# Two attention heads' kernels in one launch: another order of the first loads, and another rule for which engine copies

## The chip, the cores and the metric

The kernel runs on one core of one Trainium2 chip. A core has five engines with instruction queues of their own: PE (matrix multiplies; PEld is its weight load), DVE (vector), ACT (scalar, with table functions such as Exp), POOL (GpSimd) and SP (issues DMAs here). They wait for each other through semaphores. SBUF is the working memory of 128 partitions; PSUM, which PE writes, has 8 banks of 128 x 512 float32. The metric is the device time of one launch in microseconds (us), lower is better.

## The reference

Two blocks over inputs of 2048 rows by 512 columns, 32 heads of 16 columns each, their outputs side by side:

```python
def _A_ref(x, wqkv, wo):
    ...
    scores = jnp.einsum("bhqd,bhkd->bhqk", q, k) * scale
    p = _softmax(scores, axis=-1)
    o = jnp.einsum("bhqk,bhkd->bhqd", p, v)
    return ... @ wo
def _B_ref(x, wqkv, w_phi, wo):
    ...
    pq = jnp.einsum("bhsd,hdf->bhsf", q, w_phi)
    pk = jnp.einsum("bhsd,hdf->bhsf", k, w_phi)
    phi_q = jnp.concatenate([_softmax(pq, axis=-1), _softmax(-pq, axis=-1)], axis=-1)
    phi_k = jnp.concatenate([_softmax(pk, axis=-1), _softmax(-pk, axis=-1)], axis=-1)
    ...
    o = num / den
    return ... @ wo
return jnp.concatenate([a, b], axis=-1)
```

Block A, full softmax attention over 2048 x 2048 scores for each of 32 heads, is nearly all of the work; B is attention with linear cost.

## The kernel before

The kernel computes A's scores twice. Once with queries on the partitions (line L1050), in blocks of 128 queries by 512 keys, for which DVE takes the row maximum out of PSUM (L1058, one or two banks at once). The maxima, negated, are then put into spare rows of the query tile QT, so that the second time, with keys on the partitions (L1144), the scores come out with the maximum already subtracted, and ACT takes Exp into pT (issued in the helper at L402). PE multiplies pT with V (L1210) and with ones for the sums. There are 2048 blocks on either side. They are grouped in units: four heads by 128, 256 or 512 queries. The maxima of a unit must be complete before its first Exp; DVE runs ahead of ACT by what the code calls the lead. For the first four units a part of the maxima is taken pairwise: the score difference of two key chunks (L969), Relu by ACT, and an add with maximum on DVE (L1004).

At the start x is loaded to SG (L489), turned by PE with an identity matrix (L619, copied out by ACT and DVE in turn, L627), and then K and Q are projected: K for the first two groups by `proj_kq` (PE L533, ACT writes KT), Q for the first 128 and the next 384 queries by `first_q` (PE L575, DVE L582 and ACT). The first score block needs both. K's mask columns (kmask, kone) and the identity are made by POOL. `load_w` (L485) loads the weights' first columns: K's on SP's queue, Q's on ACT's. Later projections, block B's work and the output projections are "jobs", run by PE between the scores; copies out of PSUM follow on ACT.

No order is written out by hand. While the program is built, a planner walks through an estimated time of its own and gives each engine its next instruction: for PE in `try_pe` (queued work, then maxima or exps by how full DVE's and ACT's queues are, then products with V, jobs, and last fillers, matmuls of ones with zeros that keep the activity of PE at a set share, L1446, L1461, L1468), for the others in `try_eng` (lowest `prio` first). A copy by ACT may have an alternative on DVE (`n.alt`); `try_eng` gives it to DVE when all maxima are done or when the lead is over `K.LEAD` units. The planner's weights (`_Knobs.SPAN`) are drawn anew for each 36 us of its time, from a seed in `SEEDS0`.

Of the kernel before, what the change touches and what calls it, by code (L numbers as in the profile page):

```python
# [139 lines left out]

P0 = 0.5
W0 = 0.4


class _Knobs:
    SPAN = (("FILL", FM, FL, FH), ("FROW", 0.1, 0.0, 0.2), ("FDUP", 0.0, -0.03, 0.05), ("LCOL", 0.03, 0.0, 0.08),
# [3 lines left out]
            ("PC", 0.03, 0.0, 0.2), ("DS", 0.3, 0.05, 0.7), ("WE", W0, 0.1, 0.8), ("JN", 0.0, -0.05, 0.05),  # L150
# [30 lines left out]
def bass_concat_heads__softmax_full_mha__linear_kernel_hedgehog__prompt_kernel(  # L181
# [10 lines left out]
    RING = 28  # L192
    DT = 36
    KM = 2
    JT = 18
    SEG = 36
    SEEDS0 = [339, 17, 597, 940, 351, 78996, 101, 127, 545, 311, 973669, 597, 812, 52566, 422803204, 815, 523,
              407, 428, 535419061790, 532, 532941, 587, 227, 532591402781660, 622774033, 610, 622774292, 587,
              48, 23, 550, 382, 177996]
    VB = 7  # L200
# [20 lines left out]
    with contextlib.ExitStack() as es:  # L221
# [156 lines left out]

        log = []

        def start(n):
# [73 lines left out]
        def parity(dst, t, key, src, prio):  # L455
            pool(lambda e: e.tensor_tensor(pt4[:], t[:, 0:4], t[:, 4:8], ALU.add), 0.22, [src], ["pt4"], prio=prio)
            pool(lambda e: e.tensor_tensor(dst[:], pt4[:, 0:2], pt4[:, 2:4], ALU.add), 0.22, ["pt4"], [key],
                 prio=prio)

        blocks(hmask, "hmask", 15, 0)  # L460
        parity(kmask, hmask, "kmask", "hmask", 0)
# [26 lines left out]
        for t in range(4):  # L488
            dma("xn%d" % t, lambda e, t=t: e.dma_start(SG[:, t, :], A_x[0][128 * t:128 * t + 128, :]), (),  # L489
                [("SG", t)], prio=0, us=0.45, land=3.2, q="act" if t % 2 else "sp")  # L490
# [16 lines left out]
        pool(lambda e: e.memset(ident[:], 1.0), 0.1, (), ["ident"], prio=0)  # L507
        pool(lambda e: e.affine_select(
            ident[:], ident[:], pattern=[[-1, 128]], base=0, channel_multiplier=1,
            compare_op=ALU.is_ge, fill=0.0), 0.3, (), ["ident"], prio=0)  # L510
        pool(lambda e: e.affine_select(
            ident[:], ident[:], pattern=[[1, 128]], base=0, channel_multiplier=-1,
            compare_op=ALU.is_ge, fill=0.0), 0.3, (), ["ident"], prio=0)

# [504 lines left out]
        def try_m1_of(u, sm, single):  # L1019
# [403 lines left out]
        def try_fill():  # L1423
# [34 lines left out]
            if mode != "full":  # L1458
                if not pe_ok("col"):
                    return False  # L1460
                pe_op([lambda e, q=q: e.matmul(  # L1461
                    PS[32 * q:32 * q + 32, VB, :], ones_t[:, 0:32], zmv[:, :],
                    tile_position=(0, 32 * q), **kw) for q in range(4)], vdeps, "col")
            else:
                if not pe_ok("full"):
                    return False
                cw = 128 if now < COLD else 512
                pe_op([lambda e: e.matmul(PS[:, VB, 0:cw], ones_t[:, :], zmv[:, 0:cw], **kw)], vdeps, "full", None, (),  # L1468
                      cw / 2400.0)
# [6 lines left out]
        def try_pe():  # L1476
# [8 lines left out]
            if m1["u"] >= NU:  # L1485
# [9 lines left out]
                if pv_soon():  # L1495
                    return False
            for e in (("dve", "act") if d <= a + K.DA else ("act", "dve")):
                if e == "dve" and d < K.TM and try_m1(d < K.DS):
# [110 lines left out]


        def to_dve(n, w):
            now = state["now"]
            return r1_nodes and m1["u"] < NU and now > 1040.0 and lead() > 0.5 and free["dve"] <= w + 0.5

        def try_eng(k):
            now = state["now"]
            best = None
            for n in waiting[k]:
                w = n.when()
                if w is not None and w <= now + 1e-6 and (  # L1620
                        best is None or (n.prio, n.seq) < (best.prio, best.seq)) and not (
                            k == "act" and n.alt is not None and to_dve(n, w)):
                    best = n
            if k == "dve" and (m1["u"] >= NU or lead() > K.LEAD):
                for n in waiting["act"]:
# [5 lines left out]
                if best is not None and best.eng == "act":  # L1631
                    waiting["act"].remove(best)
                    best.eng = "dve"
                    best.run, best.occ, best.lat = best.alt
                    waiting["dve"].append(best)
# [127 lines left out]
```

## Time and profile before

| | us |
|---|---|
| three executions | 1238.96, 1210.88, 1210.67 |
| median | 1210.88 |
| the profiled execution | 1211.18 |
| its span, first to last instruction | 1209.4 |

The granted TensorE clock of that execution is 1.000. In the profile, instructions that are merged in one row have a start, a length and a count; a name such as `KT<-PS` is tile written, tile read; the number behind `<-` in brackets is idle time and who ended it. The costliest group beside those shown further down is ACT's Exp of 128 x 512 elements, 2038 times, 1055.6 us in total. The mean of a row includes the part by which an instruction overlaps the next on its engine.

### The profile page before, as it was taken

The numbers are of one execution on the slowest core, as the hardware profiler recorded it, in microseconds if no ns is written. First come the engines' busy times: TensorE is split into PE (matmuls) and PEld (weight loads), VectorE is DVE, ScalarE is ACT, GpSimd is POOL, SyncE is SP. The second block draws the span as 40 slices with busy tenths as digits, with TensorE's granted clock in tenths as the row PEclk, the third lists the DMA queues.
The fourth block names the chain that finished last, engine by engine and source line by source line (L and its number), as shares of the span: only waits on it lengthen the run. The fifth ranks groups of instructions, "written<-read, shape, count | busy, mean of one in ns | idle before, by whom it ended". The sixth has DMA issues, their size and how long they took to land.

```text
span 1209.4 us, 39536 instructions
## 1 busy us (share of the span) xinstructions
PE 1186.3 (98%) x16833; PEld 569.1 (47%) x16833; DVE 1173.3 (97%) x1195; ACT 1174.2 (97%) x2393; POOL 838.9 (69%) x1193
## 2 busy tenths in 40 slices
PE   8999999999999999999999999999999999999998
PEld 4453344444434444455444344545445434455565
DVE  6999999999999999999999999999999999999993
ACT  7899999999999999999999999999999999999998
POOL 5168988879876676678888979889898896311120
PEclk9999999999999999999999999999999999999999
DMA  9200010001000100010111211111111111000000
GB/s 201 41 12 6 7 26 9 8 7 26 9 11 22 27 7 8 9 25 17 27 32 36 46 23 33 35 26 25 25 26 26 28 40 24 14 13 9 10 12 21
DMA packets 98561, 30.48 MB, mean 25 GB/s; under 512 B 85328, under 2 KB 98384, under 8 KB 98384
## 3 DMA queue, kind: packets, MB, share of 16 engines
q1 hardware_dynamic: 97424, 27.49, 11.9%
q8 instruction: 132, 2.16, 0.7%
q10 hardware_dynamic: 960, 0.46, 0.1%
q14 instruction: 45, 0.37, 0.1%
HBM read 4.73 MB, written 4.19 MB: 7 GB/s over the span
## 4 chain that ended last, share of the span: by engine, by line
ACT 48%; PE 28%; DVE 22%; POOL 1%; issue 1%; DMA 0%; ACTq 0%; DVEq 0%; POOLq 0%
ACT pT L402 42%; DVE part L1058 21%; PE PS L1144 8%; PE PS L1050 5%; PE PS L1446 4%; PE PS L1210 3%; PE PS L533 2%; ACT eB L402 2%; PE PS L701 1%; ACT pB L402 1%; PE PS L607 1%; PE PS L1461 1%; ACT xAT L402 1%; ACT X L402 1%; PE PS L778 1%
## 5 line engine op out<-in xcount | busy, mean ns | idle before, releaser
L1058 DVE TENSOR_REDUCE part<-PS 128x2 f32<-128x1024 f32 (+1 forms) x1043 | 1146.6, 1169 | 9.3 <-PE PS L1050 3.8
L402 ACT ACTIVATE pT<-PS 128x512 bf16<-128x512 f32 x2038 | 1055.6, 692 | 15.5 <-PE PS L1144 9.3
L1144 PE MATMUL PS<-QT,KT 32*128 32x256 bf16 (+1 forms) x4480 | 696.9, 262 | 8.6 <-ACT pT L402 1.3
L1446 PE MATMUL PS<-zmv,ones_t 32*128 32x256 bf16 x3638 | 583.2, 271 | 1.1 <-ACT pB L402 0.7
L1050 PE MATMUL PS<-KT,QT 32*128 32x512 bf16 x2533 | 483.9, 382 | 3.5 <-DVE part L1058 1.7
L1144 PEld LDWEIGHTS PS<-QT,KT 32*128 32x128 bf16 x4480 | 241.7, 92 | 271.3 <-ACT pT L402 187.5
L1446 PEld LDWEIGHTS PS<-zmv,ones_t 32*128 32x128 bf16 x3638 | 275.3, 92 | 36.0 <-ACT X L402 3.6
L1210 PE MATMUL PS<-pT,VP 128*17 128x256 bf16 (+1 forms) x4480 | 193.3, 265 | 1.2 <-ACT xAT L402 0.4
L1050 PEld LDWEIGHTS PS<-KT,QT 32*128 32x128 bf16 x2533 | 124.1, 91 | 123.7 <-issue 51.5
L1271 POOL TENSOR_TENSOR lr<-lr,cons 128x8 f32<-128x8 f32 (+1 forms) x66 | 104.7, 1587 | 43.6 <-DMA lr<-X 43.5
L1210 PEld LDWEIGHTS PS<-pT,VP 128*17 128x17 bf16 x4480 | 69.1, 88 | 95.0 <-issue 81.6
L821 POOL TENSOR_TENSOR den_t<-den_t,cons 128x32 f32<-128x32 f32 x16 | 87.2, 5448 | 0.2
L741 POOL TENSOR_TENSOR sB<-eB 128x512 f32<-128x512 bf16 x32 | 36.9, 1152 | 58.6 <-ACT eB L402 58.6
L728 POOL TENSOR_SCALAR sB<-sB 128x256 f32<-128x256 f32 (+2 forms) x96 | 68.8, 717 | 6.5
L1108 POOL TENSOR_SCALAR stage<-mrow 128x8 bf16<-128x8 f32 (+1 forms) x64 | 15.3, 240 | 82.0 <-DVE mrow L1084 81.7
L1281 POOL TENSOR_TENSOR QT<-X,Yd 128x256 bf16<-128x256 f32 (+1 forms) x66 | 45.8, 693 | 35.4 <-DMA Yd<-Yd 35.4
L764 POOL TENSOR_TENSOR wA<-eB,rB 128x1024 bf16<-128x1024 bf16 x32 | 61.7, 1927 | 11.7 <-ACT rB L402 11.6
L726 POOL TENSOR_TENSOR sB<-uB 128x256 f32<-128x256 f32 (+2 forms) x96 | 45.7, 476 | 5.8
L570 POOL TENSOR_SCALAR KT<-SG,kmask,kone 128x512 bf16<-128x512 bf16 x27 | 20.5, 769 | 30.0 <-ACT SG L402 30.0
L730 POOL TENSOR_TENSOR uB<-sB,uB 128x256 f32<-128x256 f32 x64 | 37.8, 591 | 3.4
L744 POOL TENSOR_TENSOR sB<-sB 128x256 f32<-128x256 f32 x64 | 36.1, 563 | 3.1
L1461 PE MATMUL PS<-zmv,ones_t 128*32 128x512 bf16 x408 | 36.9, 386 | 0.0
(131 smaller groups left out, 866.9 us busy)
## 6 DMA issues: line engine op xcount, KB each, us to landing
Yd<-Yd SPq DMA_DIRECT2D x232, 16.0 KB, 2.1
out_dram<-xAT SPq DMA_DIRECT2D x16, 128.0 KB, 1.7
out_dram<-OA SPq DMA_DIRECT2D x15, 128.0 KB, 1.7
QT<-mcols SPq DMA_DIRECT2D x116, 2.0 KB
QT<-in_A_x_dram SPq DMA_DIRECT2D x2, 512.0 KB, 6.7
mcols<-stage SPq DMA_TRANSPOSE x64, 2.3
lr<-X SPq DMA_DIRECT2D x58, 4.0 KB
Yd<-lr SPq DMA_DIRECT2D x58, 4.0 KB
```

Source lines behind the costliest of these rows:

```text
L402: n = mk("act", lambda ds: P.op("act", lambda e: e.activation(out_(), in_(), func, **kw), ds), reads, writes, deps, occ=c + (0.093 if sbuf ...
L728: pool(lambda e, w=w: e.tensor_scalar(sB[:, 0:64 * w], sB[:, 0:64 * w], 1.0, 0.0, ALU.mult, ALU.max), us1, ["sB"], ["sB"])
L764: pool(lambda e: e.tensor_tensor(phiB[k].rearrange("p (g f) -> p g f", f=16), e3, rB[:, i, :].unsqueeze(2).broadcast_to([128, 64, 16]), AL ...
L821: pool(lambda e: e.tensor_tensor(den_t[:, :], den_t[:, :], cons[:, 0:32], ALU.pow), 5.42, ["cons"], ["den"])
L1050: fns = [lambda e, rr=rows[i], b=banks[i]: e.matmul(PS[:, b, :], QT[32 * rr:32 * rr + 32, g, q0 + 128 * qt:q0 + 128 * qt + 128], KT[32 * r ...
L1058: d = dve(lambda e: e.tensor_reduce(part[:, ub, off + m:off + m + k], PS[:, banks[0]:banks[-1] + 1, :], AX.X, ALU.max), 512 * k, (), (), d ...
L1144: fns = [lambda e, kt=kg * ns + j, j=j: e.matmul(PS[:, bank, j * nq:(j + 1) * nq], KT[32 * r:32 * r + 32, g, kt * 128:(kt + 1) * 128], QT[ ...
L1210: fns.append(lambda e, r=r, s=s, kt=kt, j=j: e.matmul(PS[32 * r:32 * r + 17, VB, 0:nq], VP[:, kt, 8 * (g // 2) + 2 * r + g % 2, :], pT[:, ...
L1271: pool(lambda e: e.tensor_tensor(lr[:, ub, 0:nr], lr[:, ub, 0:nr], cons[:, 0:nr], ALU.pow), 0.17 * nr + 0.2, ["cons"], [("lr", ub)], prio=2)
L1281: mul_nodes[u] = pool(lambda e, a=a: e.tensor_tensor(QT[:, g, q0 + a:q0 + a + w], X[:, ub, a:a + w], Yd[:, ub, a:a + w], ALU.mult), w * 0. ...
L1446: n = pe_op([lambda e, r=r: e.matmul(PS[:, VB, 0:FW], ones_t[32 * r:32 * r + 32, :], zmv[32 * r:32 * r + 32, 0:FW], tile_position=(32 * r, ...
L1461: pe_op([lambda e, q=q: e.matmul(PS[32 * q:32 * q + 32, VB, :], ones_t[:, 0:32], zmv[:, :], tile_position=(0, 32 * q), **kw) for q in rang ...
```

## The change

Five edits go together:

1. The three POOL instructions that make the identity stand ahead of the masks (they stood after the loads), all with the same `prio`.
2. Q's first weights go to SP's queue, behind K's, instead of ACT's. The K projection of the first two groups gets a lower (earlier) due time, -0.6, than Q's -0.5.
3. While the planner's time is under 20 us (`WT`), if a maximum's score block could start on PE within 0.21 us and DVE is about free, `try_pe` issues nothing else.
4. Fillers stay 128 columns wide until 9.0 us (`CW`) instead of 6.5.
5. A copy changes from ACT to DVE when the work that ACT has left exceeds DVE's by more than `K.SH` us, drawn between -1 and 9 (`behind`), and no more by the lead.

The planner's estimates of some times (load landings, identity steps) are changed too, and `SEEDS0` is another list, so all later order is planned afresh.

```diff
+S0 = 4
...
-            ("TA", 3.0, 1.2, 3.0), ("LB", 1.7, 0.6, 2.4), ("LEAD", 1.5, 1.0, 2.5), ("DA", 0.4, -0.4, 1.0),
+            ("TA", 3.0, 1.2, 3.0), ("LB", 1.7, 0.6, 2.4), ("SH", S0, S0 - 5.0, S0 + 5.0), ("DA", 0.4, -0.4, 1.0),
...
+    OT = 148
+    WT = 20
+    KF = 1
+    CW = 9.0
...
-    SEEDS0 = [339, 17, 597, 940, 351, 78996, 101, 127, 545, 311, 973669, 597, 812, 52566, 422803204, 815, 523,
+    SEEDS0 = [825, 789, 964, 663, 278, 663475996, 876, 847819, 103, 666322, 337517, 337517559, 666322306588,
...
+            if n.eng == "act":
+                if n.prio == 4:
+                    tally["e"] += len(n.frees)
+                else:
+                    tally["other"] += n.occ
             for pool, b in n.frees:
+                if pool == "m":
+                    tally["m"] += 2 if len(n.frees) == 1 and n.occ > 0.61 else 1
...
+        pool(lambda e: e.memset(ident[:], 1.0), 0.1, (), ["ident"], prio=0)
+        pool(lambda e: e.affine_select(
...
         blocks(hmask, "hmask", 15, 0)
...
-                [("SG", t)], prio=0, us=0.45, land=3.2, q="act" if t % 2 else "sp")
-        load_w("wk0", ("wA", 1, 0), 512, 640, 4.4, "sp", 0)
-        load_w("wq0", ("wA", 0, 0), 0, 128, 4.4, "act", 0)
+                [("SG", t)], prio=0, us=0.45, land=2.7, q="act" if t % 2 else "sp")
+        load_w("wk0", ("wA", 1, 0), 512, 640, 4.6, "sp", 0)
+        load_w("wq0", ("wA", 0, 0), 0, 128, 5.1, "sp", 0)
...
-        proj_kq("k", 0, 0, 0, True)
+        proj_kq("k", 0, 0, -0.6 if KF else 0, True)
...
             if not pe_ok("row", rows):
+                state["turn"] = now < WT and free["dve"] <= now + 0.5 and pe_ok("row", rows, 0.21)
                 return False
...
-                cw = 128 if now < COLD else 512
+                cw = 128 if now < CW else 512
...
+            if state["turn"]:
+                return False
...
+        def behind():
+            rd = (2048 - tally["m"]) * 0.577 + 22.0
+            ra = (2048 - tally["e"]) * 0.5 + (OT - tally["other"] - tally["given"]) * 1.045 + 7.0
+            return ra - rd
...
-            if k == "dve" and (m1["u"] >= NU or lead() > K.LEAD):
+            if k == "dve" and (m1["u"] >= NU or now > 60.0 and behind() > K.SH):
```

More of the change, by code (lines that the diff above doesn't have):

```diff
@@ L196, in bass_concat_heads__softmax_full_mha__linear_kernel_hedgehog__prompt_kernel @@
     SEG = 36
-    SEEDS0 = [339, 17, 597, 940, 351, 78996, 101, 127, 545, 311, 973669, 597, 812, 52566, 422803204, 815, 523,
-              407, 428, 535419061790, 532, 532941, 587, 227, 532591402781660, 622774033, 610, 622774292, 587,
-              48, 23, 550, 382, 177996]
+    SEEDS0 = [825, 789, 964, 663, 278, 663475996, 876, 847819, 103, 666322, 337517, 337517559, 666322306588,
+              666322306588120, 666322306588376472, 666322306588376815, 807296, 16, 799, 861, 532, 941384, 677,
+              404790, 464774, 182, 81133, 662514, 409, 520, 372, 914753986, 592, 956003]
     VB = 7
@@ L379, in bass_concat_heads__softmax_full_mha__linear_kernel_hedgehog__prompt_kernel @@
         log = []
+        tally = {"m": 0, "e": 0, "other": 0.0, "given": 0.0, "extra": 0.0}
         def start(n):
@@ L458, in parity @@
                  prio=prio)
+        pool(lambda e: e.memset(ident[:], 1.0), 0.1, (), ["ident"], prio=0)
+        pool(lambda e: e.affine_select(
+            ident[:], ident[:], pattern=[[-1, 128]], base=0, channel_multiplier=1,
+            compare_op=ALU.is_ge, fill=0.0), 0.2, (), ["ident"], prio=0)
+        pool(lambda e: e.affine_select(
+            ident[:], ident[:], pattern=[[1, 128]], base=0, channel_multiplier=-1,
+            compare_op=ALU.is_ge, fill=0.0), 0.2, (), ["ident"], prio=0)
         blocks(hmask, "hmask", 15, 0)
@@ L505, in bass_concat_heads__softmax_full_mha__linear_kernel_hedgehog__prompt_kernel @@
             load_w("wa%d" % i, key, lo, lo + (512 if lo == 1024 else 384), 9.0, "sp", 0.65)
[L507 to L513, printed above, removed]
         wo_v = A_wo.rearrange("(a r b d) n -> r b d a n", r=4, b=2, d=16)
@@ L1496, in try_pe @@
                     return False
+            state["turn"] = False
             for e in (("dve", "act") if d <= a + K.DA else ("act", "dve")):
@@ L1633, in try_eng @@
                     best.eng = "dve"
+                    tally["given"] += best.occ
+                    tally["extra"] += best.alt[1]
                     best.run, best.occ, best.lat = best.alt
```

## The prediction, made before the run

> **What bounds the kernel now.** I read the page first: span, engine totals, shares of the chain of waits.
>
> ```profile
> span 1209.4 us, 39536 instructions
> PE 1186.3 (98%) x16833; PEld 569.1 (47%) x16833; DVE 1173.3 (97%) x1195; ACT 1174.2 (97%) x2393; POOL 838.9 (69%) x1193
> ACT 48%; PE 28%; DVE 22%; POOL 1%; issue 1%; DMA 0%; ACTq 0%; DVEq 0%; POOLq 0%
> ```
>
> DVE and ACT are equally full, so totals don't say which sets the end; PE's 98% contains filler matmuls and decides nothing. I therefore asked for the busy time by stage (columns: stretch, its length, PE, PEld, DVE, ACT, POOL), cutting at DVE's first maximum, at 60 us, and after its last maximum, and then for the waits of DVE and of ACT between 60 and 1150 us.
>
> ```profile
> 0.00:11.00 11.00, 8.26 (x71) 6.28 (x72) 2.00 (x5) 3.84 (x6) 7.73 (x26) 1.00 0.88 211
> 11.00:60.00 49.00, 46.76 (x430) 19.23 (x430) 47.11 (x91) 44.08 (x83) 11.90 (x24) 1.00 0.55 102
> 60.00:1150.00 1090.00, 1075.95 (x15016) 508.94 (x15014) 1085.03 (x1052) 1071.69 (x2193) 810.96 (x1128) 1.00 0.10 20
> 1150.00:1187.20 37.20, 36.80 (x893) 24.04 (x886) 36.41 (x42) 36.04 (x77) 8.27 (x17) 1.00 0.06 10
> 1187.20:1209.40 22.20, 18.52 (x442) 10.60 (x439) 2.78 (x9) 18.56 (x37) 0.00 (x0) 1.00 0.09 27
> ```
>
> ```profile
> DVE part L1058 <- PE PS L1144: 1.6, 7, 0.4
> DVE part L1058 <- PE PS L1446: 0.8, 3, 0.4
> DVE part L1058 <- PE PS L1050: 0.6, 2, 0.5
> ```
>
> ```profile
> ACT pT L402 <- PE PS L1144: 7.3, 18, 1.3
> ```
>
> Between 60 and 1150 us DVE idles 1090.00 - 1085.03 = 5.0 us, ACT 18.3 us, and ACT's largest wait is for scores that need a finished row maximum. So DVE, running the maxima, is the bound from 11 to 1187 us. ACT follows it and owns only the last 22.2 us. The time is: start until DVE's first maximum (11 us), DVE's work with 1.9 + 5.0 + 0.8 = 7.7 us of pauses, and ACT's tail. An edit pays if it shortens one of these three.
>
> **The start.** The next rows are the timeline from zero (start, length, engine, line); the first DVE row is the first maximum, the second one ends DVE's first pause. Below them stand two stretches by engine and DMA issues with microseconds to landing.
>
> ```profile
> 0.82 0.87 ACTq L489 DMA_DIRECT2D SG<-in_A_x_dram  x2
> 1.70 0.43 SPq L485 DMA_DIRECT2D wA<-in_A_wqkv_dram  x1
> 1.72 0.46 ACTq L485 DMA_DIRECT2D wA<-in_A_wqkv_dram  x1
> 1.76 2.66 PE L1468 MATMUL PS<-zmv,ones_t 128*128 128x128 bf16 x23
> 2.78 0.29 POOL L511 TENSOR_SCALAR_AFFINE_SELECT ident<-ident 128x128 bf16<-128x128 bf16 x1
> 4.22 1.50 PE L619 MATMUL PS<-ident,SG 128*128 128x128 bf16 x16
> 5.31 1.29 DVE L627 CAST xAT<-PS 128x512 bf16<-128x512 f32 x2 [5.31 <-PE PS L619]
> 7.41 0.40 PE L575 MATMUL PS<-xAT,wA 128*128 128x128 bf16 x4 [1.69 <-DMA wA<-in_A_wqkv_dram]
> 7.64 1.03 PE L1468 MATMUL PS<-zmv,ones_t 128*128 128x512 bf16 x4
> 7.84 0.74 DVE L582 TENSOR_SCALAR QT<-PS,kmask 128x128 bf16<-128x128 f32 x2 [1.25 <-PE PS L575]
> 8.51 1.03 PE L533 MATMUL PS<-xAT,wA 128*128 128x512 bf16 x4
> 9.37 0.81 PE L575 MATMUL PS<-xAT,wA 128*128 128x384 bf16 x4
> 9.64 0.78 ACT L402 ACTIVATE KT<-PS,kone,kmask 128x512 bf16<-128x512 f32 x1 [3.51 <-PE PS L533]
> 10.56 0.39 PE L1050 MATMUL PS<-KT,QT 32*128 32x512 bf16 x2
> ```
>
> ```profile
> 10.99 3.71 DVE L1058 TENSOR_REDUCE part<-PS 128x2 f32<-128x1024 f32 x3 [2.41 <-PE PS L1050]
> 15.40 6.01 DVE L1058 TENSOR_REDUCE part<-PS 128x2 f32<-128x1024 f32 x5 [0.70 <-PE PS L1050]
> ```
>
> ```profile
> 17.51 1.20 ACT L402 ACTIVATE uB<-PS 128x512 f32<-128x512 f32 x2
> ```
>
> ```profile
> 10.00:15.00 5.00, 4.33 (x46) 2.50 (x43) 3.58 (x3) 5.00 (x11) 3.21 (x8) 1.00 0.96 262
> 15.00:20.00 5.00, 4.92 (x28) 1.59 (x27) 4.52 (x4) 5.00 (x10) 1.23 (x4) 1.00 1.15 239
> ```
>
> ```profile
> SG<-in_A_x_dram ACTq DMA_DIRECT2D x2, 128.0 KB, 2.8
> wA<-in_A_wqkv_dram SPq DMA_DIRECT2D x1, 128.0 KB, 5.2
> wA<-in_A_wqkv_dram ACTq DMA_DIRECT2D x1, 128.0 KB, 5.6
> ```
>
> Now, K's first weights land at 1.70 + 5.2 = 6.9 us, but PE is then parked in front of Q's, from ACT's queue, until 7.41; Q's projection and four long fillers run before K's, at 8.51. K's evacuation at 9.64 ends the wait of everything. In the changed program, as built, PE runs twelve fillers (twelve of 23 in 2.66 us: until 3.15), the sixteen transposes, thirteen fillers, K's projection, three fillers, Q's two projections, one filler, and four score matmuls.
>
> *Identity first.* The identity is done at 2.78 + 0.29 = 3.07 now, and the fillers hold the transposes until 4.22. With it third in POOL's queue it is done by about 2.1 (an estimate: its three steps take the place of the masks'), the fillers by 3.15, and x lands about 0.82 + 2.8 = 3.6: the transposes go from 3.6 to 5.1, their last copy ends near 6.0 instead of 6.60. That alone buys nothing, because the weights land at 6.9. Behind it on POOL, the mask of ones slides behind the long memset of VP; it is done near 6.2 us by the same steps, 1.9 us before K's evacuation needs it.
>
> *K first, in one queue.* The thirteen fillers end by 5.1 + 13 x 0.116 = 6.6, under the landing at 6.9. K's projection runs from about 6.95 to 7.98, its evacuation starts at 8.08: 9.64 - 8.08 = 1.56 us sooner. Q's weights, issued at 2.13 on SP instead of 1.72 on ACT, land between 2.13 + 5.2 = 7.3 and 2.13 + 5.6 = 7.7, and are needed at about 8.2. The x and transpose issues behind them on SP come 0.43 us later. Further down SP's queue the eight loads of WOp now stand ahead of W3, for which POOL's block masks wait; POOL is busy for 11.9 of the 49 us there, so I count nothing. The Q projection, last before the scores, ends about 9.2, so that scores start at 9.25 and the first maximum at 9.25 + 0.43 = 9.7 instead of 10.99: 1.3 us. From 10 to 20 us ACT has no idle time, and K's chunks and the Relu copies on which DVE's next maxima hang come from it, so its 1.56 us carry; I take 1.5 for the start. Bounds: 0 if the weights land late by that much, and 2.0 if ACT's first Relu copy, now at 17.51, gains the 1.56 and also the one SG copy put behind it (about 0.5).
>
> The Trainium skill, in "DMA: Bandwidth & Descriptors", section "Queues, rings and completion order", has each DMA engine take turns between queue rows and work through one row in order. By that, K's weights would land before 6.9, Q's no longer taking turns with them. The fillers in front end at 6.6, so the sum would be better by at most 0.3; no row here shows it.
>
> *Early scores claim TensorE.* Where a score pair would be possible within 0.21 us in the first 20 us, PE now waits instead of taking other work. It can remove at most the pause of 0.70 before 15.40. What waits behind it on PE are K's later projections and, through them, ACT's copies. I count zero: two K projections and eight transposes now stand between the fourth and fifth pair, which can make a pause there of the same size.
>
> **Copies by work left.** The built program has these counts. Before 60 us nothing differs in kind. After it DVE takes 2 copies (one pB, one xAT, at two thirds of the run) instead of 5 (two pB, two X, one vB, at about 200 us), and 15 pair maxima are split into 30 single ones.
>
> ```profile
> L1058 DVE TENSOR_REDUCE part<-PS 128x1 f32<-128x512 f32 x86 | 54.4, 681 | 1.7 <-PE PS L1144 1.0 <-PE PS L1446 0.2
> L406 DVE COPY X<-PS 128x256 f32<-128x256 f32 x2 | 0.8, 420 | 0.0
> L406 DVE CAST vB<-PS 128x512 bf16<-128x512 f32 x1 | 0.7, 683 | 0.0
> L1058 DVE TENSOR_REDUCE part<-PS 128x2 f32<-128x1024 f32 x957 | 1095.4, 1213 | 7.6 <-PE PS L1050 3.8 <-PE PS L1144 1.2 <-PE PS L1446 0.9
> ```
>
> ```profile
> 1158.79 9.05 DVE part L1058 x8
> ```
>
> ```profile
> 1200.95 2.45 ACT pT L402 x5
> ```
>
> A pair in a row costs 9.05 / 8 = 1.13 us, 0.08 less than its 1.213, which is overlap. A single so costs 0.60, a 512-wide copy 0.60, a 256-wide 0.34. Splitting adds 15 x (1.20 - 1.13) = 1.05 us to DVE; the copies take away 3 x 0.60 + 2 x 0.34 - 2 x 0.60 = 1.28. DVE's work falls by 0.2. ACT gets three copies, at most 3 x 0.5 = 1.5 us, which its 18.3 us of idle time hold; without that cover they would cost 1.5. In the tail, 36 score blocks follow the last maximum on PE instead of 34: two exps at 2.45 / 5 = 0.49, less one OA copy that goes to DVE: +0.5.
>
> **Sum.** -1.5 - 0.2 + 0.5 = -1.2 us. The profiled execution took 1211.18 (span 1209.4, 1.8 around it), 0.3 over the median of 1210.88. Against the median: 1209.7. DVE's 7.7 us of pauses I leave as they are: the new seeds draw all of the plan's weights afresh, which may shrink or widen them.
>
> **Rivals.**
> - *The redrawn plan also closes DVE's pauses.* DVE's waits for PE, of up to 0.5 us each, are a maximum whose matmul stands behind other matmuls, and order can cure that. Half of 7.7 gone is 3.9 more: 1205.8. For it, the lead of issued maxima over issued exps stays higher in the changed program (52 to 38 blocks at the 1408th exp); against it, short waits in a full PE queue tend to move rather than go.
> - *Slower: K's projections starve DVE.* Between fourth and fifth pair stand two projections of 1.03 and eight transposes (0.75 by the sixteen), 2.8 us in which DVE holds at most one pair more, 1.13: a pause of 1.7, 1.0 more than 0.70. A third projection stands between the sixth pair and the first Relu sum: 1.03. Together +2.0, hence 1211.7. It decides if ACT's evacuations keep these projections from starting before DVE has drained its pairs.
> - *Slower by a slow PE start.* The first fillers cost 116 ns for 128 columns, the later ones 1.03 / 4 = 0.26 for 512. If PE dropped to the first pace in the new, shorter filler groups, K's projection would take 1.85 (+0.8), Q's last 1.39 (+0.6), the transposes 1.86 (+0.4): +1.8, 1211.5. Against it: PE stood still from 5.72 to 7.41 now, and the fillers after it still ran at the quick pace; the new pauses are shorter. The Trainium skill, "TensorE: Matmul & The Clock Gate", section "Part 1: The HAM clock gate (the "warmup" mystery)", has the clock at half rate until a window of about 3.4 us was busy, with the window running free; by that rule this falls out differently from run to run, and the quick fillers agree with it.
> - *It doesn't do what it says:* Q's or x's landing slips by the 1.5 us: 1211.2.
>
> **Numbers.** Forecast 0.47 (own range 1208.3 to 1211.0), closed pauses 0.25, starved DVE 0.16, slow PE 0.06, late landing 0.06. The range goes from 0.8 below the closed pauses (all 7.7 gone would be 1202) to 1.3 above the dearer of the slower cases, the end to which a mix of the two would tend. Two per cent, about what a measurement of this kernel can tell from no change, is 24 us; no case reaches that. For an execution of the kind of the 1238.96 seen before I keep 0.03 on the slow side, 0.01 on the fast one, 0.96 between.
>
> **What would show it.** K's evacuation at 8.1 us and the first maximum at 9.7; ACT's first uB copy near 16; DVE idle near 5 us between 60 and 1150; 22 to 23 us after the last maximum. Wrong if K's projection waits past 7.5, if a DVE pause of over 1.5 us appears before 20 us, or if ACT idles less than DVE between 60 and 1150: then copies, not maxima, set the time.

## The result, and the profile after

| | before | after |
|---|---|---|
| median of six executions, us | 1210.85 | 1206.33 |
| lowest and highest | 1210.67, 1238.96 | 1205.63, 1208.94 |
| the profiled execution | 1211.18 | 1205.91 |
| its span | 1209.4 | 1204.2 |

The ratio of the times is 0.996, with a 95% interval of 0.9948 to 0.9973 (the one execution of 1238.96 is left out of it): the changed kernel is 4.5 us faster, well inside two per cent. The forecast was 1.2 us faster, and the rival with closed pauses 5.1.

First the page of the changed kernel: span, engine totals, shares of the chain of waits.

```profile
span 1204.2 us, 39322 instructions
PE 1166.6 (97%) x16665; PEld 568.6 (47%) x16754; DVE 1171.6 (97%) x1208; ACT 1174.4 (98%) x2395; POOL 840.3 (70%) x1193
ACT 42%; DVE 30%; PE 26%; issue 1%; DMA 0%; DVEq 0%
```

PE is busy 19.7 us less (some of it because records are missing: 16754 weight loads stand against 16665 matmuls), and DVE and ACT are as full as they were; in the chain some of ACT's share has gone to DVE. Nothing here says where 5.2 us went. For that I cut the span at the same events as before: DVE's first maximum, 60 us, 1150 us, the last maximum. Below are the busy times by stage of the changed kernel (stretch, length, PE, PEld, DVE, ACT, POOL, then the granted clock, the DMA share and GB/s), the last row being the whole stretch from the first maximum to the last, and then that stretch of the kernel before.

```profile
0.00:8.88 8.88, 7.41 (x67) 5.64 (x68) 2.09 (x5) 3.69 (x5) 7.65 (x26) 1.00 0.85 216
8.88:60.00 51.12, 47.33 (x438) 19.98 (x445) 49.37 (x94) 46.49 (x89) 13.32 (x24) 1.00 0.60 107
60.00:1150.00 1090.00, 1062.93 (x14945) 512.42 (x15021) 1085.55 (x1066) 1074.45 (x2201) 813.30 (x1130) 1.00 0.11 20
1150.00:1181.35 31.35, 30.93 (x764) 19.79 (x762) 31.03 (x35) 30.51 (x64) 6.05 (x13) 1.00 0.06 11
1181.35:1204.20 22.85, 17.96 (x476) 10.80 (x469) 3.57 (x11) 19.28 (x39) 0.00 (x0) 0.99 0.08 25
8.88:1181.35 1172.47, 1141.19 (x16140) 552.19 (x16227) 1165.95 (x1193) 1151.44 (x2353) 832.67 (x1167) 1.00 0.13 24
```

```profile
10.99:1186.95 1175.96, 1159.27 (x16322) 552.01 (x16321) 1168.37 (x1181) 1151.57 (x2352) 831.14 (x1168) 1.00 0.12 23
```

The 5.2 us of span fall into three parts. The start: 8.88 instead of 10.99, -2.1. From first to last maximum: 1172.47 instead of 1175.96, -3.5. The tail: 22.85 instead of 1209.40 - 1186.95 = 22.45, +0.4. Within the middle part DVE's visible idle time fell only from 7.6 to 6.5 us; its busy time fell by 2.4.

The timeline of the start of the changed kernel (start, length, engine, line; in brackets the idle time before and who ended it) shows the first part.

```profile
3.65 1.87 PE L632 MATMUL PS<-ident,SG 128*128 128x128 bf16 x16 [0.40 <-DMA SG<-in_A_x_dram]
5.32 1.06 PE L1482 MATMUL PS<-zmv,ones_t 128*128 128x128 bf16 x13
6.39 1.02 PE L546 MATMUL PS<-xAT,wA 128*128 128x512 bf16 x4
7.42 1.04 PE L588 MATMUL PS<-xAT,wA 128*128 128x128 bf16 x8
7.52 1.59 ACT L415 ACTIVATE KT<-PS,kone,kmask 128x512 bf16<-128x512 f32 x2 [1.73 <-PE PS L1482]
8.45 0.39 PE L1064 MATMUL PS<-KT,QT 32*128 32x512 bf16 x4
8.88 4.62 DVE L1072 TENSOR_REDUCE part<-PS 128x2 f32<-128x1024 f32 x4 [0.21 <-PE PS L1064]
14.51 2.35 DVE L1072 TENSOR_REDUCE part<-PS 128x2 f32<-128x1024 f32 x2 [1.02 <-PE PS L1064]
15.17 0.61 ACT L415 ACTIVATE uB<-PS 128x512 f32<-128x512 f32 x1
```

```profile
wA<-in_A_wqkv_dram SPq DMA_DIRECT2D x2, 128.0 KB, 4.5
```

K's projection starts at 6.39 with no wait for a DMA in front of it, its evacuation at 7.52, the first maximum at 8.88. The two weight loads, now in one queue, land after 4.5 us by the median; in two queues they took 5.2 and 5.6. The pause before the fifth pair is 1.02 us, and ACT's first uB copy comes at 15.17 instead of 17.51.

For the middle part I looked at the waits of DVE and ACT from 60 to 1150 us, and at DVE's groups by shape (count, then busy us, mean ns, idle before).

```profile
DVE part L1072 <- PE PS L1158: 1.8, 8, 0.3
DVE part L1072 <- PE PS L1064: 0.7, 3, 0.3
DVE part L1072 <- PE PS L1460: 0.6, 2, 0.4
ACT pT L415 <- PE PS L1158: 5.8, 18, 1.1
```

```profile
L1072 DVE TENSOR_REDUCE part<-PS 128x2 f32<-128x1024 f32 x942 | 1076.2, 1213 | 5.0 <-PE PS L1158 2.0 <-PE PS L1064 1.8 <-PE PS L1460 0.6
L1072 DVE TENSOR_REDUCE part<-PS 128x1 f32<-128x512 f32 x116 | 72.1, 681 | 0.9 <-PE PS L1064 0.2
```

The waits that the profile can name are nearly what they were: 1.8 us behind the exps' scores (before 1.6), 0.7 behind the maxima's own (0.6) and 0.6 behind fillers (0.8). But a pair maximum now takes 1076.2 / 942 = 1.1425 us of DVE, before 1095.4 / 957 = 1.1446, and a single 0.622 instead of 0.633. Two maxima overlap by 0.08 us where the second is ready in time; one that comes late by less than that loses overlap, and no idle time is seen. Start to start, the undisturbed pair takes 1.131 and the single 0.598 in both kernels; with these the forecast's 15 splits and three copies fewer make -0.3, and what is left of the 3.5 us, 3.2 to 3.3, is pauses, 1.1 of them seen as idle.

Where along the way it happens is told by the end of the nth block maximum (of 2024 on DVE: 942 x 2 + 116 in pairs and singles, and 24 sums of the pairwise part), after less before, in us:

| n | 2 | 20 | 50 | 100 | 200 | 500 | 1000 | 1300 | 1700 | 2000 | 2024 |
|---|---|---|---|---|---|---|---|---|---|---|---|
| us | -2.11 | -1.99 | -2.33 | -3.13 | -4.06 | -7.53 | -6.80 | -7.90 | -4.51 | -4.75 | -5.60 |

The start's gain stands by n = 2 and is kept. Of the rest, 2.1 us are there by n = 200. The swings behind that are work done at another time: the kernel before gives its five copies to DVE between n = 377 and 424, the changed one runs 51 of its singles between n = 1536 and 1664. To take these out, call lost time what DVE takes from its first maximum to the start of the nth beyond 1.131 us for each pair, 0.598 for each single, 0.60 or 0.34 for each copy, and its other instructions as they ran (in us):

| n | 50 | 100 | 150 | 200 | 400 | 1000 | 2024 |
|---|---|---|---|---|---|---|---|
| before | 2.1 | 2.9 | 3.4 | 4.5 | 6.3 | 8.4 | 14.3 |
| after | 1.9 | 1.9 | 1.9 | 2.4 | 3.6 | 6.2 | 11.4 |

By this count the pauses shrink by 2.8 us, and nearly all of that is there at n = 400, about 245 us into the span. From there to the end the difference moves between 1.5 and 3.3 and doesn't grow.

### The profile page after: what moved, and what is told of

The parts are those of the page before. It is cut to its first block, busy times and chain, and to the rows that moved or that the text cites. A ratio compares the mean times of both kernels' runs of the same rounds, so it can differ in the third digit from the quotient of the medians.

```text
span 1204.2 us, 39322 instructions
## 1 busy us (share of the span) xinstructions
PE 1166.6 (97%) x16665; PEld 568.6 (47%) x16754; DVE 1171.6 (97%) x1208; ACT 1174.4 (98%) x2395; POOL 840.3 (70%) x1193
## 4 chain that ended last, share of the span: by engine, by line
ACT 42%; DVE 30%; PE 26%; issue 1%; DMA 0%; DVEq 0%
ACT pT L415 37%; DVE part L1072 30%; PE PS L1158 8%; PE PS L1064 4%; PE PS L1460 4%; PE PS L1224 4%; ACT eB L415 1%; PE PS L855 1%; ACT pB L415 1%; PE PS L546 1%; PE PS L714 1%; ACT xAT L415 1%; ACT X L415 1%; PE PS L1475 1%; PE PS L842 0%
## 5 line engine op out<-in xcount | busy, mean ns | idle before, releaser
L1460 PE MATMUL PS<-zmv,ones_t 32*128 32x256 bf16 x3577 | 571.9, 271 | 0.1
L1064 PE MATMUL PS<-KT,QT 32*128 32x512 bf16 x2503 | 478.9, 382 | 6.6 <-DVE part L1072 4.5
L1460 PEld LDWEIGHTS PS<-zmv,ones_t 32*128 32x128 bf16 x3577 | 271.6, 92 | 34.2 <-ACT X L415 2.7
```

The costliest lines, as they stand in the source:

```text
L1064: fns = [lambda e, rr=rows[i], b=banks[i]: e.matmul(PS[:, b, :], QT[32 * rr:32 * rr + 32, g, q0 + 128 * qt:q0 + 128 * qt + 128], KT[32 * r ...
L1460: n = pe_op([lambda e, r=r: e.matmul(PS[:, VB, 0:FW], ones_t[32 * r:32 * r + 32, :], zmv[32 * r:32 * r + 32, 0:FW], tile_position=(32 * r, ...
```

## The experiments

Four kernels plan afresh: a1 is the kernel before with the new seeds, a2 to a4 are the changed kernel with one group of edits undone. Two leave the plan alone and change queues of the changed kernel's finished program, with the waits worked out anew (f1, f2). Two more put additional work into it (f3, f4), and one changes the start of the finished program of the kernel before (g3). Three others are told as they come. The kernel before ran beside each; its medians there were 1211.18 to 1211.40, 0.3 to 0.6 above the 1210.85 beside which the changed kernel ran; differences to the changed kernel's 1206.33 below may be too large by that.

**The start alone.** In the finished program of the kernel before, Q's weights go behind K's on SP, and PE's order between the Q projection and the first scores is changed to fillers, K, Q, scores, transposes. All that follows is as it was.

```diff
+        lens = (("Q", 4), ("F", 4), ("K", 4), ("Q2", 4), ("X", 8), ("S", 2))
...
+        order = [i for name in ("F", "K", "Q", "Q2", "S", "X") for i in piece[name]]
...
+        pi[i0:p] = [pi[i] for i in order]
...
+        sp_items.insert(at + 1, ac.pop(w))
```

> The kernel before, its finished program unchanged but for the start: Q's weights behind K's on SP's queue; on PE the four long fillers, then K's projection, Q's two, the first score pair, and then the first eight transposes of the next chunk. If a start carries one to one to the end: K's evacuation near 7.8 us, first maximum near 9.3 instead of 11.0, end earlier by the same 1.5 to 1.8 us: 1209.3 us. If DVE's first pause or ACT takes it up: less than half of that, 1210.4 or more.

Median 1210.97 against 1211.40, ratio 0.9994 (0.9986 to 1.0003). The timeline of this kernel's start:

```profile
7.27 0.78 ACT L402 ACTIVATE KT<-PS,kone,kmask 128x512 bf16<-128x512 f32 x1 [1.66 <-PE PS L533]
9.41 1.22 DVE L1058 TENSOR_REDUCE part<-PS 128x2 f32<-128x1024 f32 x1 [1.25 <-PE PS L1050]
11.30 2.35 DVE L1058 TENSOR_REDUCE part<-PS 128x2 f32<-128x1024 f32 x2 [0.67 <-PE PS L1050]
14.36 6.01 DVE L1058 TENSOR_REDUCE part<-PS 128x2 f32<-128x1024 f32 x5 [0.70 <-PE PS L1050]
```

The first maximum comes 1.58 us sooner, but the second pair now waits 0.67 us behind the transposes, so that the maxima from the fourth pair on, at 14.36 instead of 15.40, are 1.04 sooner. That difference is there at the end too. The last group of maxima, first in this kernel and then in the one before:

```profile
1181.19 4.69 DVE L1058 TENSOR_REDUCE part<-PS 128x2 f32<-128x1024 f32 x4
```

```profile
1182.24 4.70 DVE L1058 TENSOR_REDUCE part<-PS 128x2 f32<-128x1024 f32 x4
```

The span is 1.0 shorter (1208.4). From the fourth pair's start to the end of the last maximum it takes 1171.52 us in this kernel and 1171.54 in the one before, so in the profiled executions the 1.04 that is left there arrives whole. The medians show less: their difference of 0.4 falls in the second case that was expected (1210.4 or more), and its interval still holds none and 1.7.

**K's weights late.** In the finished changed program K's load goes behind Q's and the first large load of x; nothing else is touched.

```diff
+        sp_items = P.streams["sp"].items
+        at = {k: i for i, (_, _, k) in reversed(list(enumerate(sp_items)))}
+        sp_items.insert(at["d_xn8"], sp_items.pop(at["d_wk0"]))
```

> The finished program with K's first weights issued on SP behind Q's and the first of the two 512 KB loads of x: about 1.0 us later in issue, landing 1 to 3 us later. If DVE's first maximum sets all that follows, the end moves by as much as the first maximum moves, within 0.5 us: 1207 to 1209.5 us. If later pauses absorb a late start, less than half of the shift is seen at the end.

Median 1211.31 (1210.25 to 1215.52), ratio to the kernel before 1.0000 (0.9992 to 1.0009): all of the gain is lost. Rows of its start and of its last maxima from the timeline, and its page's span:

```profile
9.79 1.89 PE L546 MATMUL PS<-xAT,wA 128*128 128x512 bf16 x4 [3.79 <-DMA wA<-in_A_wqkv_dram]
14.39 4.62 DVE L1072 TENSOR_REDUCE part<-PS 128x2 f32<-128x1024 f32 x4 [1.11 <-PE PS L1064]
1183.27 3.48 DVE L1072 TENSOR_REDUCE part<-PS 128x2 f32<-128x1024 f32 x3
```

```profile
span 1209.6 us, 39322 instructions
```

The changed kernel's last group of maxima is this one:

```profile
1177.86 3.48 DVE L1072 TENSOR_REDUCE part<-PS 128x2 f32<-128x1024 f32 x3
```

The first maximum is 5.51 us later, the last 5.41, the span 5.4. So a late start goes through one to one in this plan; g3 shows the same for the plan before, in the other direction, from the fourth pair on and by its traces only. The shift was larger than expected: K's projection starts 3.40 us later, and after PE had stood for 3.79 us, it took 1.89 us instead of 1.02, Q's projections behind it 1.91 instead of 1.04, and so on up to the first maximum, together 2.1 more.

**Q's weights back on ACT's queue**, again in the finished program.

```diff
+        sp_items = P.streams["sp"].items
+        at = {k: i for i, (_, _, k) in reversed(list(enumerate(sp_items)))}
+        P.streams["act"].items.insert(2, sp_items.pop(at["d_wq0"]))
```

> The changed kernel's finished program, with one issue moved: Q's first weights go out on ACT's queue as before, and nothing else of any engine's order differs. If the shared queue is what lets K's weights land early (the turn-taking of queue rows), K's projection starts near 6.9 us instead of 6.39 and the first maximum comes 0.3 to 0.5 us later: 1206.7 us. If the landing doesn't depend on the queue: 6.4 us, no change (1206.3).

Median 1206.78 (1206.22 to 1209.54), 0.45 over the changed kernel's, with ranges that overlap. DMA issues with median us to landing, and two rows of its start:

```profile
wA<-in_A_wqkv_dram ACTq DMA_DIRECT2D x1, 128.0 KB, 5.4
wA<-in_A_wqkv_dram SPq DMA_DIRECT2D x1, 128.0 KB, 5.2
```

```profile
5.19 1.59 PE L1482 MATMUL PS<-zmv,ones_t 128*128 128x128 bf16 x13
6.91 1.05 PE L546 MATMUL PS<-xAT,wA 128*128 128x512 bf16 x4
```

K's weights land at 1.70 + 5.2 = 6.9, just as in the kernel before, and K's projection starts then, 0.52 later than in the changed kernel. The landing times agree with the turn-taking of the Trainium skill, "DMA: Bandwidth & Descriptors", section "Queues, rings and completion order". But the 13 fillers ahead were also slow in this execution (1.59 us for 1.06), and so they were in another kernel (f4, below) with one queue. What of the 0.52 is the queue and what the clock isn't separated, and its effect on the time, at most some tenths, is within the spread.

**Rules and seeds exchanged.** The kernel before with the new seeds:

```diff
-    SEEDS0 = [339, 17, 597, 940, 351, 78996, 101, 127, 545, 311, 973669, 597, 812, 52566, 422803204, 815, 523,
+    SEEDS0 = [825, 789, 964, 663, 278, 663475996, 876, 847819, 103, 666322, 337517, 337517559, 666322306588,
...
```

> The kernel before, with the changed kernel's seeds. Theory A (the start comes from the edits, DVE's shorter pauses from the new list of seeds): K's evacuation still near 9.6 us and DVE's first maximum near 11.0, but pauses between first and last maximum like the changed kernel's 6.5 us instead of 7.6 by busy time: 1207 to 1209 us. Theory B (a list of seeds only fits the plan for which it was picked; with other rules it is just another draw): pauses of 9 us or more, 1212 to 1217 us.

and the changed kernel with the old ones (the same two lines exchanged):

> The changed kernel with the old list of seeds. Both theories: K's evacuation near 7.5 us, first maximum near 8.9. Theory A: pauses like before, so only the start's 2.1 us and about 0.2 of DVE's work are gained: 1208 to 1209 us. Theory B: a random draw under new rules, pauses of 9 us or more: 1210 to 1215 us, slower than or equal to before in spite of the earlier start.

The first took 1233.01 (ratio 1.0173, 1.0113 to 1.0232), the second 1223.91 (1.0117, 1.0085 to 1.0149). One row by stage of each, first of a1, then of a2; the figure behind POOL is the granted clock:

```profile
710.00:730.00 20.00, 19.81 (x218) 8.34 (x218) 15.98 (x17) 15.64 (x33) 16.41 (x20) 0.66 0.10 21
```

```profile
83.00:91.00 8.00, 8.00 (x54) 3.03 (x50) 5.63 (x7) 5.44 (x11) 3.66 (x5) 0.57 0.05 7
```

Both are above all that was expected (up to 1217 and 1215). Neither the edits with other seeds nor the seeds with the old rules keep the time, and part of the loss stands in stretches where PE is busy throughout at little over half its clock, and DVE and ACT starve. a2 has the new start (first maximum at 8.83) and is still 17.6 us slower than the changed kernel: the start is 2 us, and the plan can cost much more than that. Part of a1's loss is its start: PE's first 126 matmuls are those of the kernel before, but Q's weights landed at 7.67 us instead of 7.41, and then PE was slower.

```profile
7.67 0.61 PE L575 MATMUL PS<-xAT,wA 128*128 128x128 bf16 x4 [2.54 <-DMA wA<-in_A_wqkv_dram]
8.07 1.91 PE L1468 MATMUL PS<-zmv,ones_t 128*128 128x512 bf16 x4
12.68 3.71 DVE L1058 TENSOR_REDUCE part<-PS 128x2 f32<-128x1024 f32 x3 [3.62 <-PE PS L1050]
```

The four fillers took 1.91 us instead of 1.03, and the first maximum comes at 12.68 instead of 10.99. a3, below, has the same first 126 matmuls and its first maximum at 14.57.

**The old start with the new rule and seeds.** Identity, queue, due time, `WT`, `CW` and landing estimates as before; only the rule for copies and the seeds are new.

```diff
-    WT = 20
-    KF = 1
-    CW = 9.0
+    WT = 0
+    KF = 0
+    CW = 6.5
...
-        load_w("wq0", ("wA", 0, 0), 0, 128, 5.1, "sp", 0)
+        load_w("wq0", ("wA", 0, 0), 0, 128, 4.4, "act", 0)
```

> The changed kernel with its start undone (identity behind the loads, Q's weights on ACT's queue, K's projection not ahead, no claim on TensorE, short fillers to 6.5 us, old landing estimates), new copy rule and new seeds. Theory A: K's evacuation back near 9.6 us, 2.1 us lost: 1208 to 1209 us. Theory B: as the plan differs from the first microseconds on, the seeds no longer fit, and more than 2.1 is lost: 1210 to 1215 us.

**The old rule for copies with the new start and seeds.**

```diff
-            if k == "dve" and (m1["u"] >= NU or now > 60.0 and behind() > K.SH):
+            if k == "dve" and (m1["u"] >= NU or lead() > K.LEAD):
```

> The changed kernel with the old rule for copies (by the lead) and everything else new. If the copy rule itself matters, the lead rule gives DVE three or more copies more, 0.6 us each: 1207 to 1209 us with the first 200 us unchanged. If plans behind the point where they part are just other draws (theory B): pauses of 9 us or more, 1209 to 1214 us.

a3 took 1230.72 (ratio 1.0172, 1.0114 to 1.0231), a4 1254.74 (1.0326, 1.0280 to 1.0372). a4's busy time by stage around its worst stretch:

```profile
480.00:490.00 10.00, 9.67 (x118) 4.01 (x116) 9.61 (x13) 10.00 (x23) 7.12 (x10) 1.00 0.07 13
490.00:550.00 60.00, 60.00 (x556) 30.23 (x555) 40.85 (x36) 39.15 (x73) 19.53 (x31) 0.50 0.07 14
550.00:560.00 10.00, 9.92 (x140) 4.34 (x134) 9.10 (x9) 9.56 (x19) 8.66 (x12) 0.91 0.05 9
```

The granted clock is halved for 60 us, and DVE idles 19 us of them. These two are above all that was expected as well (up to 1215 and 1214). So the times of these four don't tell what each edit is worth: a different edit makes a different plan, and the medians of the four plans are 18 to 48 us above the changed kernel's.

The first 260 us tell more, for there (from 15 us on) the granted clock is 1.00 in a1, a3 and a4 as in the two kernels. DVE's lost time at n = 200 and n = 400, counted as above, is 4.5 and 6.3 us in the kernel before and 2.4 and 3.6 in the changed one; a1 has 2.6 and 4.7, a3 3.2 and 6.5, a4 2.2 and 3.6. So the new seeds under the old rules (a1) already bring 1.6 of the 2.7 us gained by n = 400, without the new rule for copies all of it is there (a4), and with the old start none of it at n = 400 (a3).

**The same plan for half of the way.** The changed kernel with the old seeds from the 18th entry on. Its DVE instructions are the same up to about the middle.

```diff
-    SEEDS0 = [825, 789, 964, 663, 278, 663475996, 876, 847819, 103, 666322, 337517, 337517559, 666322306588,
+    SEEDS0 = [825, 789, 964, 663, 278, 663475996, 876, 847819, 103, 666322, 337517, 337517559, 666322306588, 666322306588120, 666322306588376472, 666322306588376815, 807296, 407, 428, 535419061790,
...
```

> The changed kernel with the old list of seeds from its 18th entry on: the instructions are the same up to 638 on DVE (about the middle), the rules are the same throughout. Theory B (a plan is a draw, and the picked one is a good one): the first half as in the changed kernel, the pauses in the second half longer by 3 to 10 us, with halved clock somewhere: 1210 to 1225 us. If the rules and not the draw make the pauses: within 2 us of 1206.3.

Median 1220.36 (1214.90 to 1226.47), ratio 1.0077 (1.0049 to 1.0104). From 60 to 600 us, first this kernel and then the changed one:

```profile
60.00:600.00 540.00, 524.46 (x7240) 248.31 (x7282) 538.04 (x520) 532.03 (x1092) 415.00 (x609) 1.00 0.08 14
```

```profile
60.00:600.00 540.00, 524.47 (x7240) 248.33 (x7282) 538.04 (x520) 531.97 (x1092) 415.31 (x609) 1.00 0.08 14
```

The two agree there to the hundredth on PE and DVE. In its profiled execution (span 1213.2) the last maximum then ends 4.3 us later than in the changed kernel and the tail is 27.5 us instead of 22.85. Nothing differs but the draws of the second half, and they decide 9 us in that execution, 14 in the medians. The lost time gained by n = 400 is still gained here (4.0 us, before 6.3): what is lost is lost behind it.

**No copies to DVE before the last maximum**, the seeds kept:

```diff
-            if k == "dve" and (m1["u"] >= NU or now > 60.0 and behind() > K.SH):
+            if k == "dve" and m1["u"] >= NU:
```

> The changed kernel in which no copy goes from ACT to DVE before the last maximum. The instructions are the same up to 826 on DVE (about two thirds), then two copies stay on ACT. By the work moved alone: DVE 1.2 us less, ACT 1.0 us more: 1205 to 1207.5 us. Theory B, a new draw behind that point: pauses longer by 2 to 8 us, 1208 to 1220 us.

Median 1217.28 (1209.16 to 1249.86); the seven of ten executions at a clock of 0.985 or more have a median of 1211.74, and with them the ratio to the kernel before is 1.0018 (0.9993 to 1.0044). DVE's order is the same up to its 826th instruction. From 800 to 1000 us DVE idles 3.5 us at a clock of 0.98, in the changed kernel 0.7 at 1.00, and the tail is 24.7. The price of the rule for copies can't be read from it, since the plan behind the first copy is drawn otherwise too.

**Does filling hold the clock?** In a4's finished program, the fillers of 32 rows that were planned between 400 and 660 us and after 1150, 1001 of them, are issued twice.

```diff
+            fn, need, key = pi[i]
+            pi[i:i + 1] = [(fn, need, None), (fn, {}, key)]
```

> The finished program with the lead rule (the one of 1254.7 us, whose clock was halved for 61 us from 490 us on), in which 1001 of the small filler matmuls, those of the plan's 400 to 660 us and after 1150 us, are issued twice. If the halved clock is what costs, and too little work on PE ahead of 490 us brings it: no long half-clock stretch there, the clock 0.99 or more, 1217 to 1225 us. If the plan's own pauses cost and the clock only follows them: 1245 us or more.

Median 1398.42 (1372.53 to 1431.24), mean granted clock of the profiled execution (1380.72) 0.926. By stage:

```profile
440.00:460.00 20.00, 20.00 (x293) 14.65 (x289) 15.14 (x13) 16.33 (x32) 13.44 (x18) 1.00 0.03 6
480.00:500.00 20.00, 20.00 (x180) 11.19 (x177) 8.93 (x9) 9.63 (x18) 7.49 (x15) 0.50 0.03 5
```

The theory that the clock falls for want of fillers did not hold. With twice as many PE is the bound at full clock already (DVE idles 4.9 of 20 us), and the clock falls all the same. What brings it down stays open.

**What a few more instructions cost.** In the finished changed program, ten more maxima of 512 columns of a constant tile on DVE, spread over the middle; and, in another, ten more copies of 512 columns on ACT. Both write spare memory.

```diff
+            dv.insert(300 + 51 * i, (lambda e, i=i: e.tensor_reduce(
+                spare_d[:, i:i + 1], zmv[:, :], AX.X, ALU.max), {}, None))
```

> The finished program with ten extra maxima over 512 columns of a constant tile put into DVE's stream between about 250 and 850 us, with no wait and nobody waiting for them: 0.6 us each. If DVE's work sets the time between first and last maximum: +5 to +6 us, 1211.5 to 1212.3. If ACT sets it, DVE's slack takes them: under +2 us.

```diff
+            av.insert(700 + 110 * i, (lambda e, i=i: e.activation(
+                BD[:].rearrange("p a b -> p (a b)"), zmv[:, :], ACT.Copy), {}, None))
```

> The finished program with ten extra copies of 512 columns of a constant tile put into ACT's stream between about 340 and 830 us, with no wait and nobody waiting for them: about 0.5 us each. If DVE sets the time, ACT's idle time takes them: under +1 us, 1206.3 to 1207.3. If ACT sets it as much as DVE does: +4 to +5 us, 1210.5 to 1211.3.

On DVE: median 1210.44 (1209.85 to 1221.95), 4.1 over the changed kernel, of 10 x 0.60 = 6.0 put in: between the two cases that were expected. On ACT: 1211.81 (1209.81 to 1220.59), 5.5 over it. Both have executions at a lower clock, down to 0.986 and 0.989. The seven of twelve at 0.999 or more have medians of 1210.15 and 1210.33, against 1206.12 for such executions of the changed kernel: 4.0 and 4.2 more. f3's profiled execution (1219.38) is one at a lower clock, so only f4's is read here. From f4's profile, its group of extra copies and its stretch from 60 to 1150 us:

```profile
L1737 ACT ACTIVATE BD<-zmv 128x512 bf16<-128x512 bf16 x10 | 7.1, 707 | 0.0
```

```profile
60.00:1150.00 1090.00, 1061.33 (x14849) 509.01 (x14923) 1083.36 (x1063) 1075.04 (x2202) 812.10 (x1127) 1.00 0.11 20
```

At full clock, the profiled span is 1208.6, 4.4 us more, 0.6 of it from a later start (first maximum at 9.52). So some 3.8 us reach the end. What was put on ACT is 6.9 us, more than the 0.48 that an exp of the same size takes in a row: from the start of the exp ahead to such a copy it is 0.65 us instead of 0.48, and 0.52 from the copy to what follows, together 0.69 for each. ACT was idle for 15.5 us of this stretch in the changed kernel, and is idle for 15.0 here: the copies did not go into the idle time, they pushed other work of ACT out of the stretch, and DVE lost 2.2 us of busy time. An engine that isn't the bound by its idle time charged 3.8 / 6.9, a good half, of what was added; the bound itself charged 4.0 / 6.0.

## Why the prediction was right, and where it was off

The time, 1206.3, lies in the range and within 2% of before, 3.4 below the forecast. It lies outside the forecast's own range (1208.3 to 1211.0), 0.5 from the rival with closed pauses, which had a chance of 0.25: the range held because that rival was in it. Two of the three terms came out within 0.1 us and the start within 0.6; DVE's pauses, whose change was set to zero, made up most of the difference.

- *What bounds the kernel.* DVE as the bound, ACT owning the tail: ten more maxima on DVE cost 4.1 us (f3), so DVE does count. But to tell the bound by which engine idles less was too sharp a reading: ten more copies on ACT cost about as much (f4), though ACT idles 15.5 us from 60 to 1150 us and DVE 4.5. The sign "if ACT idles less than DVE" could not have shown that.
- *The start, -1.5: the mechanism was right, and the size is the term that was mis-sized.* It measured -2.1 at the first maximum and -2.0 at the 20th. K's projection started at 6.39 instead of the 6.95 that I took from the old landing; the sentence on the Trainium skill's rule for queues allowed 0.3 of that, and the quick fillers let the rest be used. From K's evacuation to the first maximum it took 1.36 us, not 1.62. That a shift at the first maximum goes through to the end is shown by f2. The bound of 2.0 was passed by 0.1. The size compares one execution of each kernel: the same old start gave first maxima at 10.99 (before), 12.68 (a1) and 14.57 us (a3), the new one between 8.37 (g2) and 9.54 (g1), so in other executions the start may be worth more.
- *Early scores.* Counted at zero. A pause before the fifth pair came as described, 1.02 us in place of the 0.70 ahead of the fourth, and no other behind it. The edit by itself was not tried.
- *DVE's work, -0.2.* By the durations that hold in both kernels it is -0.3.
- *ACT's idle time holds three more copies.* This step was wrong as reasoned. By f4's price, 0.38 us for a copy, the three cost up to 1.1 us, and about 0.8 if the price goes by time on ACT, 0.48 against 0.69 (estimates; f4's copies were put in without the planner). PE works through one fixed order in which scores for DVE and scores for ACT alternate and wait for each other's banks; that this is how a late ACT delays DVE is argued from the kernel's order, and f4 shows only the price.
- *The tail, +0.5.* Measured +0.4.
- *DVE's pauses, unchanged.* This is the step that failed in size: they shrank by 2.8 to 3.3 us, near the 3.9 of the rival with chance 0.25, and mostly as overlap that the idle times of the profile don't show. Hence the 7.7 us from which I took half was the wrong base: the lost time at the last maximum was 14.3, a fifth of it went, and that its size came close to half of 7.7 is luck. Nearly all of the gain is made in the first 245 us. There the rule for copies has no part in it (a4), and the new seeds bring 1.6 of 2.7 us without any other edit (a1). Whether the start's edits bring the rest stays open, and so does what in the new order closes the pauses. That the gain lasts to the end belongs to the draws behind it: with the first 600 us equal and other draws after, the kernel is slower than before (g2).
- *The starved DVE* (a pause of 1.7 before the fifth pair, another before the Relu sums): the pause was 1.02, the second did not come, and the start was earlier by more. *The slow PE start*: PE was at the quick pace for K's projection here; f2 shows that the mechanism exists (1.89 us after a standstill), as the rival priced it. a1 and a3 show it in the old start, behind standstills of 2.54 and 3.05 us; the new start has no standstill over 0.3 us at that place. Of the kernel before 22 executions took 1212 to 1214 us; whether a start of this kind made them, no trace shows. *A late landing* did not occur; f2 made one, and it costs what it shifts.
- *The chance of slower, 0.03.* The line that no case reaches 24 us overlooked that a fresh draw may give a plan in which the clock falls: five other plans, drawn under these or the old rules (a1 to a4, g2), were all slower than the kernel before, by 0.8 to 3.3%; a sixth, g4, was 0.2% slower with an interval that holds none, and took up to 1249.86. No row of the profile of before could tell the draw, but the range of its results was missing from the rivals.

## What to carry to other kernels

When a change makes a planner draw its whole order afresh, cost the edit and the draw apart: the edit by its stage, the draw by what other draws of the same planner give, whose medians here were 14 to 48 us above the plan that was kept (five plans) and 5 in the mildest case (g4 without its executions at a low clock), while the earlier start was worth 2. A shift of the first instruction of the bound went through to the end here, and such a shift can be tested without a new plan by reordering the finished queues. Idle time of an engine in totals need not be cover for more work on it: put ten extra instructions there and read the price.

## What the runs showed of the hardware that was not expected

- The same start runs at different paces. The group of 13 fillers behind the transposes took 0.89 us in g2, 1.06 in the changed kernel and 1.59 in f1 and f4, with the same instructions ahead on PE; K's evacuation began between 7.0 us (g2) and 8.18 (g1) in programs whose start is equal. About a microsecond of the start is thus not in the program's hands. In f2, PE at the quick pace for 13 fillers (0.89 us) ran its next work at half of it after standing for 3.79 us, while in the kernel before a standstill of 1.69 left the pace as it was. This agrees with the Trainium skill, "TensorE: Matmul & The Clock Gate", section "Part 1: The HAM clock gate (the "warmup" mystery)", which has the clock follow windows of about 3.4 us of PE's activity. But standstills of 2.54 us (a1) and 3.05 (a3), shorter than such a window, were followed by the slow pace as well: the next four fillers took 1.91 us instead of 1.03.
- The granted clock falls to 0.50 in the middle of work with PE busy for 60.00 of 60 us (a4), and stayed there while more fillers were issued (g1: 0.50 with 20.00 of 20). The executions of a4 follow the mean clock: 1244.60 us at 0.970, 1255.02 and 1254.47 at 0.959 and 0.957, 1277.06 at 0.934. PE's busy time by itself does not keep the clock here.
- Two loads of 128 KB, issued one behind the other, land in a median of 3.8 (g3) to 4.7 us (a4) from one queue; one on each of two queues, they land in 5.2 and 5.4 (f1) to 5.2 and 6.3 us (a3).
- Ten copies on ACT from SBUF to SBUF in the midst of exps did not overlap the exp ahead: 0.65 us from its start to the copy's, while the kernel's copies out of PSUM into X, SG and xAT start 0.48 behind it in the median (f4).
